# FNet mixing and gated layers on one Trainium2 core: 65-row tiles for the odd folds, a padded row 512, earlier weight loads and a new place table

## The chip, the cores and the metric

The kernel runs on one core of a Trainium2 chip. The metric is the device time of that core in microseconds (us), the median of 3 runs. The core's engines are the matrix engine (PE), VectorE (DVE), ScalarE (ACT), GpSimd (POOL) and SyncE (SP), which here issues nearly all the transfers, in program order on one queue.

## The reference

Two equal layers on x of 2048 rows and 640 columns, all in float32; the three weights are the same in both layers and have 1728 inner columns.

```python
for layer in range(2):
    z = layernorm(x)
    x = x + (Cr @ (z @ Hr.T) - Ci @ (z @ Hi.T))      # real part of the DFT over the rows of the DFT over the columns
    z = layernorm(x)
    x = x + (sigmoid(z @ w_gate) * (z @ w_up)) @ w_down
```

Cr and Ci are the 2048 x 2048 cosine and sine matrices of the sequence, Hr and Hi the 640 x 640 ones of the columns.

## The kernel before

**Layout.** The function `folded` does the work. It uses the symmetries of the DFT matrices, and tests the given matrices for them beside the work; a general version stands by for other inputs and isn't run here. One large buffer in the on-chip memory, `big` in the profile, holds 406 units of 128 float32 columns. Everything that comes and goes is a run of units in it: `take(n, name)` hands one out, `drop(name)` gives it back. Where each of the 913 takes lies is written in the table PLACES, in program order. A take over a place that was in use a moment before waits, by semaphores, for the last reader of the old content, so the table decides which jobs wait for which.

**Products in float16 halves.** Most operands are split into a high and a low float16 part (`split`, lines 234 to 239: ScalarE makes the high part at L237, VectorE the low one at L239), and each product is three matmuls, high x high, high x low and low x high (`PASSES`). In the opening of layer 1 the sequence step works on float32 directly.

**The mixing step.** The rows of x come in 4 quarters of 512, each as four groups GA to GD of 128 rows. Column c and column 640 - c, and row s and row s + 1024 or 2048 - s, are added and subtracted first. What comes of it are an even fold FE of 321 columns and an odd fold FO of 320 columns; the 321st column of FO is cleared (`zero_odd`, line 848, in the opening, and line 680 in `fold_join`), so that both have one width in memory. Quarter 1 (`SP`) has besides a lone row, row 512, which is its own mirror image. It is kept apart as `row`, float32 on partition 0 (lines 601 to 605), is scaled in `fold_row` and split to `fw`, and meets the cosine matrix' row 512, `cx` raw and `c512` split.

The sequence step (`sequence32`, line 812, float32, for layer 1; `sequence`, line 759, float16, for layer 2) multiplies a fold, as weights, by a sequence matrix, as moving data of 256 or 257 columns, and so transposes it: the fold's columns land on partitions, in three tiles d. `KT` (line 758) gives for each parity r the first column and the number of columns of these tiles: 128, 128 and 65 for the even fold, 128, 128 and 64 for the odd one. Row 512 is added by further matmuls with one row of contraction (K = 1): one per tile in float32 (L832), three per tile in float16 (L793).

The hidden step contracts over those same tiles, whose row counts are again `KT[r]`:

```python
def product(ps, ph, r, at, m):
    for d, (_, n) in enumerate(KT[r]):
        w = held["h", r, d].f16[:n]
        for zp, wps in PASSES:
            z = held["z", ph, d].parts[zp][:n]
            for wp in wps:
                nc.tensor.matmul(ps[:m, :EC], z[:, at : at + m], w[:, 384 * wp : 384 * wp + EC],
                                 start=(d == 0 and zp == HI and wp == HI), stop=(d == ND // 2 and zp == LO))
```

The matmul is L917, and its shape in the profile is weights n x m and moving data n x 321. One `hidden` step is two products of 9 matmuls. There are 8 of them per layer, and `hidden_middle` besides, with a single column (m = 1) for output row t = 512, which `evict_middle` reads from partition 0 of the result. The matrices' rows come from `load_wh` (first layer) and `load_wh_again`.

**The gated step.** `gate_up` (L1123) and the later `seven` and `four` (L1167, tile by tile of the inner columns, index j) make the gate and up products; ScalarE evicts them (L1171). `seven` and `four` use sums and differences of blocks, in the manner of Strassen, so that fewer products are needed; the weights' sums are made in layer 1 (`load_sums`, `make_sums`, `split_sums`, `keep_sums`) and kept in device memory (`kept_S`, `kept_G`). The down product of layer 1's first half is done directly (`down`, L1309). The others use seven forms of pairs of weight tiles (`stage`, L1423), which layer 1 prepares during its second half: for each of the six pairs n, `load_forms` loads the raw weights (L1333, L1335) to `fr`, `make_forms` makes four differences on GpSimd (L1342 and the lines after) in `ft`, `split_forms` splits three forms from `fr` (part 0) and four from `ft` (part 1) on ScalarE and VectorE, and `keep_forms` stores them to `kept_f`.

The rows for the second half of the gated step come in four row pairs i. For each, `pair_apply` normalizes, `pair_combine` makes the sums, `pair_parts` splits them in four parts (L516 on ScalarE, L517 on VectorE), and `pair_transpose` issues the transposing transfers (L533).

**What orders the work.** The first 99 us (the mixing step of layer 1 and the start of the gated step) are a list written by hand, OPENING. After that the matrix engine's steps stand in one list with planned durations; T is the sum of these, and `when(t, f, ...)` puts a job of another engine into the program at planned time t. The planned times only set the program order: within an engine, and on the queue of transfers, work goes in that order, whatever it waits for. T = 0 is at about 98.9 us of the profile. Three planned times are used below: `d0`, the start of the down product of the first half (T = 146.3, about 247 us), `s1`, the start of the second half's `seven` (T = 235.4, about 336 us), and 96 + 11.5 k, the turn of the k-th sequence matrix. These turns belong to layer 1: `load_c`, `split_c` and `stored_c` prepare the 8 sequence matrices and row 512 in float16 for layer 2, where `load_c_again` and `load_c512_again` load them.

## Time and profile before

| | |
|---|---|
| runs | 1110.03, 1113.09, 1113.80 us |
| median | 1113.09 us |
| span of the profiled execution | 1111.5 us, 17471 instructions |
| matrix engine busy | 1091.5 us (98%), 6295 instructions |
| VectorE | 828.8 us (75%) |
| ScalarE | 570.9 us (51%) |
| GpSimd | 152.1 us (14%) |

The profile is of one execution, the times are of others. In a line of the timeline stand the start in us, the duration, the engine, the source line, the operation, the tile written and read with its shape, and how often it came in a row; in brackets the idle time before it and what ended that. For a matmul the shape `65*128 65x321` means weights of 65 rows and 128 columns and moving data of 65 rows and 321 columns. "SPq" is the queue of transfers. In a row of the windows view come the stretch, its length, the time of the matrix engine, of its weight loads, of VectorE, ScalarE and GpSimd (each with the number of instructions), the granted clock of the matrix engine, the share of the DMA engines and GB/s. Matmuls overlap in the records, so the time that one takes is read from the distance of the starts.

### The profile page before, as it was taken

Reading aid. Unit: us, or ns where it says so; the run is one execution under the profiler, and the core shown is the slowest. Engines: PE = TensorE matmul, PEld = TensorE weight load, DVE = VectorE, ACT = ScalarE, POOL = GpSimd, SP = SyncE. Lnnn points to the kernel's source line nnn. Section 1 sums busy time; section 2 is a strip of 40 time slices with the busy share of each in tenths; the row PEclk is TensorE's granted clock in tenths of the full one; section 3 lists DMA queues with packets and bytes.
Section 4 is the critical chain, followed back from the end, with each engine's and each line's share of the span. In section 5 each row is a group of like instructions: output and inputs, shape, how many; then the busy total and the mean of one; then the engine's idle time right before and its main releaser. Section 6 shows DMA issues by size and latency. Waiting matters only on the chain.

```text
span 1111.5 us, 17471 instructions
## 1 busy us (share of the span) xinstructions
PE 1091.5 (98%) x6295; PEld 621.8 (56%) x6295; DVE 828.8 (75%) x1608; ACT 570.9 (51%) x1108; POOL 152.1 (14%) x245
## 2 busy tenths in 40 slices
PE   6999999999998999999999999999999999999997
PEld 3667444447774444447777744444677544444775
DVE  8986789867556999769886659885896356777952
ACT  7766447765333656546224544477553245455520
POOL 3110151321323243000020000012000010000010
PEclk9999999999999999999999999999999999999999
DMA  9413764365888778856833039645669756666611
GB/s 278 159 49 70 197 205 173 106 208 156 209 232 263 249 237 246 239 163 212 242 110 119 1 49 192 188 165 164 200 175 202 221 184 198 211 196 191 225 61 63
DMA packets 183080, 194.69 MB, mean 175 GB/s; under 512 B 76459, under 2 KB 145476, under 8 KB 182984
## 3 DMA queue, kind: packets, MB, share of 16 engines
q1 hardware_dynamic: 182344, 190.86, 58.7%
q0 software_dynamic: 640, 2.62, 0.6%
q8 instruction: 51, 0.84, 0.3%
q14 instruction: 45, 0.37, 0.1%
HBM read 145.29 MB, written 31.90 MB: 159 GB/s over the span
## 4 chain that ended last, share of the span: by engine, by line
PE 83%; DVE 6%; DMA 5%; SPq 3%; ACT 1%; issue 1%; POOL 1%; DVEq 0%; POOLq 0%; ACTq 0%
PE acc L1167 38%; PE acc L1423 17%; PE acc L1123 14%; PE acc L917 4%; PE acc L1404 3%; PE acc L1276 2%; DMA big<-in_wu 2%; PE acc L829 2%; PE acc L786 1%; SPq L533 1%; SPq L1495 1%; DMA big<-in_wd 1%; DVE big L239 1%; DMA big<-in_x 1%; DMA big<-in_ct 1%
## 5 line engine op out<-in xcount | busy, mean ns | idle before, releaser
L1167 PE MATMUL acc<-big 128*128 128x512 f16 x2160 | 469.5, 380 | 3.9 <-ACT big L1171 3.2
L1167 PEld LDWEIGHTS <-big 128*128 128x128 f16 x2160 | 211.6, 98 | 260.3 <-issue 6.1
L1423 PE MATMUL acc<-big 128*128 128x320 f16 x1512 | 213.2, 299 | 0.4 <-DVE big L1297 0.4
L1171 ACT ACTIVATE big<-acc 128x512 f32<-128x512 f32 x160 | 94.0, 592 | 181.7 <-PE acc L1167 169.8
L1423 PEld LDWEIGHTS <-big 128*128 128x128 f16 x1512 | 147.9, 98 | 58.5 <-issue 0.6
L1123 PE MATMUL acc<-big 128*128 128x512 f16 (+1 forms) x900 | 156.5, 337 | 0.0
L1123 PEld LDWEIGHTS <-big 128*128 128x128 f16 x900 | 87.8, 98 | 68.2 <-issue 0.8
L1474 ACT ACTIVATE big<-big 128x768 f32<-128x768 f32 (+6 forms) x106 | 79.0, 746 | 64.5 <-DVE big L1504 24.9
L239 DVE SCALAR_TENSOR_TENSOR big<-big 128x640 f16<-128x640 f32 (+7 forms) x94 | 75.7, 829 | 19.1 <-ACT big L237 19.0
L1297 DVE SCALAR_TENSOR_TENSOR big<-acc,big 128x320 f32<-128x320 f32 x112 | 53.1, 486 | 48.7 <-PE acc L1404 25.8
L1309 PE MATMUL acc<-big 128*128 128x320 f16 x656 | 89.3, 299 | 0.0
L237 ACT ACTIVATE big<-big 128x640 f16<-128x640 f32 (+9 forms) x94 | 63.8, 707 | 48.9 <-DMA big<-in_ct 21.9
L1384 DVE TENSOR_TENSOR big<-big 128x512 f16<-128x512 f32 x126 | 85.5, 689 | 4.4 <-ACT big L1383 4.4
L1383 ACT ACTIVATE big<-big 128x512 f16<-128x512 f32 x126 | 72.8, 616 | 18.4 <-DVE big L1261 10.1
L1309 PEld LDWEIGHTS <-big 128*128 128x128 f16 x656 | 64.2, 98 | 25.1
L1217 DVE TENSOR_TENSOR big<-big,acc 128x512 f32<-128x512 f32 x40 | 27.3, 682 | 41.0 <-PE acc L1167 26.0
L516 ACT ACTIVATE big<-big 128x384 f16<-128x384 f32 (+2 forms) x56 | 36.1, 667 | 35.4 <-DVE big L501 18.5
L1174 ACT ACTIVATE big<-big 128x512 f32<-128x512 f32 x80 | 49.7, 621 | 8.2 <-DVE big L1217 7.2
L517 DVE TENSOR_TENSOR big<-big 128x384 f16<-128x384 f32 (+2 forms) x56 | 42.6, 773 | 13.6 <-ACT big L516 13.5
L386 POOL DMA_INDIRECT out<-big,rows x8 | 8.8, 1097 | 309.2 <-DVE big L1297 168.0
L1395 DVE TENSOR_TENSOR big<-big 128x512 f32<-128x512 f32 x72 | 50.2, 699 | 0.1
L917 PE MATMUL acc<-big 128*128 128x321 f16 (+3 forms) x324 | 48.6, 300 | 0.0
(195 smaller groups left out, 1193.5 us busy)
## 6 DMA issues: line engine op xcount, KB each, us to landing
big<-in_ct SPq DMA_DIRECT2D x256, 128.0 KB
big<-kept_f SPq DMA_DIRECT2D x63, 320.0 KB
big<-kept_S SPq DMA_DIRECT2D x33, 512.0 KB
big<-kept_w SPq DMA_DIRECT2D x33, 320.0 KB
big<-in_ct SPq DMA_DIRECT2D x32, 256.0 KB
big<-kept_G SPq DMA_DIRECT2D x21, 320.0 KB
kept_S<-big SPq DMA_DIRECT2D x13, 512.0 KB
big<-in_wg SPq DMA_DIRECT2D x19, 320.0 KB
```

What stands on the lines that cost most here:

```text
L237: nc.scalar.activation(dh, src, AF.Copy, scale=s)
L239: nc.vector.scalar_tensor_tensor(dl, src, s, dh, op0=OP.mult, op1=OP.subtract)
L917: nc.tensor.matmul(ps[:m, :EC], z[:, at : at + m], w[:, 384 * wp : 384 * wp + EC], start=(d == 0 and zp == HI and wp == HI), stop=(d == ND ...
L1123: nc.tensor.matmul(ps, w[wp][:, d * P : (d + 1) * P], xt[:, xp, :], start=(d == 0 and wp == HI and xp == HI), stop=(d == ND - 1 and wp == LO))
L1167: nc.tensor.matmul(ps, wt, xt, start=start and n == 0, stop=n == len(todo) - 1, skip_group_check=not start)
L1171: nc.scalar.activation(dst, ps, AF.Copy)
L1297: nc.vector.scalar_tensor_tensor(xe, ps[:, :EH], CB, xe, op0=OP.mult, op1=OP.add)
L1309: nc.tensor.matmul(held["pd", i, e][0][:, :EH], held["t", half, j].parts[hp][:, i * P : (i + 1) * P], held["w", 2, j].parts[wp][:, e * EH ...
L1383: nc.scalar.activation(h, v, AF.Copy)
L1384: nc.vector.tensor_tensor(l, v, h, op=OP.subtract)
L1423: nc.tensor.matmul(ps[:, :EH], a[n][hp][:, i * P : (i + 1) * P], w[n][:, wp], start=fresh and m == 0, stop=m == len(todo) - 1, skip_group_ ...
L1474: nc.scalar.activation(v, v, AF.Square, accum_out=new_sum()[:p])
```

## The change

1. **Third tile of the odd folds.** `KT` gives both parities 128, 128 and 65 rows. On the sequence side the new row is the cleared 321st column; on the hidden side `load_wh` loads one more row of the odd matrix.
2. **Row t = 512.** `hidden_middle` takes 97 columns that end at the one wanted, instead of one column, and `evict_middle` reads partition 96 instead of partition 0.
3. **Row 512, padded.** `row` and `cx` are cleared on all 128 partitions on GpSimd before they are filled, and the float32 matmul in `sequence32` takes 128 rows instead of one. In float16 the parts go onto spare partitions of one cleared tile: in `fw` the high part on rows 0 and 64 and the low part on row 32, in `c512` the high part on rows 0 and 32 and the low part on row 64. One matmul with 128 rows gives the three products at once. `fw` takes 2 units instead of 3, `c512` in layer 2 takes 3 instead of 5, and is loaded by a clear and three transfers instead of one transfer. `sequence` no longer stores `c512` itself; `stored_c512` still does.
4. **Planned times, all in layer 1.** The third and fourth row pairs go from d0 + 50 and d0 + 63 to d0 + 47 and d0 + 57. The sequence matrices are loaded 4 us of plan earlier, row 512 3 us earlier. The raw weights of pair 0 are loaded at s1 - 30 instead of s1 - 12; its differences and splits stay where they are.
5. **PLACES** is a new table for the takes of this program. It is cut here to its first and last lines.

```diff
--- before.py
+++ after.py
@@ -72,39 +72,39 @@
 PLACES = """
-115 380 366 221 234 326 146 85 141 307 80 372 151 90 122 367 401 275 190 272 377 138 258 352 161 108 166 289
...
-301 372 148 332 160 336 368 276 169 203 280 295 344 208 176 243 225"""
+405 80 404 403 81 86 91 96 400 101 395 106 111 116 121 126 390 131 134 384 387 381 140 143 374 369 364 359 354
...
+273 327 208 343 402 172 367 336 237 332"""
@@ -601,7 +601,9 @@
         if i == SP:
 
             if "row" not in held:
-                take(6, "row")
+                v = take(6, "row").f32[:, :EC]
+                if not steps:
+                    nc.gpsimd.memset(v, 0.0)
             on.tensor_copy(held["row"].f32[0:1, 384 * k : 384 * k + EC], e[0:1, 1])
 
     def fold_power(i, k0, k1, on=nc.gpsimd):
@@ -649,10 +651,13 @@
             nc.vector.scalar_tensor_tensor(f[0:1, :EC], f[0:1, 384 : 384 + EC], t[0:1, GD, 19:20], f[0:1, :EC],
                                            op0=OP.mult, op1=OP.add)
         if n == 2:
-            nc.scalar.activation(take(3, "fw").f16[0:1, :EC], f[0:1, :EC], AF.Copy)
+            w = take(2, "fw").f16[:, :EC]
+            nc.gpsimd.memset(w, 0.0)
+            for p in (0, 64):
+                nc.scalar.activation(w[p : p + 1], f[0:1, :EC], AF.Copy)
         if n == 3:
-            w = held["fw"].f16
-            nc.vector.tensor_tensor(w[0:1, 384 : 384 + EC], f[0:1, :EC], w[0:1, :EC], op=OP.subtract)
+            w = held["fw"].f16[:, :EC]
+            nc.vector.tensor_tensor(w[32:33], f[0:1, :EC], w[0:1], op=OP.subtract)
             drop("row")
 
     def drop_rev():
@@ -743,7 +748,9 @@
         nc.sync.dma_start(kept_part(take_c(r, i), r), kept["c", r, i])
 
     def load_c512():
-        nc.sync.dma_start(take(5, "cx").f32[0:1, : SB + 2], ct[0, SB : SB + 1, : SB + 2])
+        v = take(5, "cx").f32[:, : SB + 2]
+        nc.gpsimd.memset(v, 0.0)
+        nc.sync.dma_start(v[0:1], ct[0, SB : SB + 1, : SB + 2])
 
     def split_c512(do=ALL):
         h, l = (held["c512"] if "c512" in held else take(5, "c512")).parts
@@ -752,9 +759,12 @@
             drop("cx")
 
     def load_c512_again():
-        nc.sync.dma_start(kept_part(take(5, "c512"))[0:1, :, :257], kept["c512",])
-
-    KT = ((0, P), (P, P), (2 * P, EC - 2 * P)), ((0, P), (P, P), (2 * P, EH - 2 * P))
+        v = take(3, "c512").f16
+        nc.gpsimd.memset(v[:, :257], 0.0)
+        for p, q in ((0, 0), (32, 0), (64, 1)):
+            nc.sync.dma_start(v[p : p + 1, :257], kept["c512",][:, q])
+
+    KT = (((0, P), (P, P), (2 * P, EC - 2 * P)),) * 2
 
     def sequence(i, tp):
 
@@ -787,17 +797,12 @@
                                              start=(i % 2 == 0 and r == 0 and xp == HI and cp == HI),
                                              stop=(i % 2 == 1 and r == 1 and xp == LO))
                     if i == SP and tp == EV and r == 0:
-                        xv, cps = held["fw"].f16[0:1], held["c512"].parts
-                        for xp, cs in PASSES:
-                            for cp in cs:
-                                nc.tensor.matmul(o, xv[:, 384 * xp + c0 : 384 * xp + c0 + n], cps[cp][0:1, :257],
-                                                 start=False, stop=False)
+                        nc.tensor.matmul(o, held["fw"].f16[:, c0 : c0 + n], held["c512"].f16[:, :257],
+                                         start=False, stop=False)
 
         def post():
             if i == SP and tp == EV:
                 drop("fw")
-                if ("c512",) not in kept:
-                    keep(kept_part(held["c512"])[0:1, :, :257], "c512")
                 drop("c512")
             summed.add((i, tp))
             if {(i, EV), (i, OD)} <= summed:
@@ -829,7 +834,7 @@
                     nc.tensor.matmul(o[:n], xv[:, c0 : c0 + n], moving(r), start=i % 2 == 0 and r == 0,
                                      stop=i % 2 == 1 and r == 1)
                     if i == SP and tp == EV and r == 0:
-                        nc.tensor.matmul(o[:n], held["row"].f32[0:1, c0 : c0 + n], held["cx"].f32[0:1, 0 : SB + 1 : 2],
+                        nc.tensor.matmul(o[:n], held["row"].f32[:, c0 : c0 + n], held["cx"].f32[:, 0 : SB + 1 : 2],
                                          start=False, stop=False)
 
         def post():
@@ -892,7 +897,7 @@
 
     def load_wh(r, d):
         s = take(3, "hr", r, d).f32
-        n = KT[1][d][1]
+        n = KT[r][d][1] - (r == 0 and d == 2)
         nc.sync.dma_start(s[:n, :EC], wh[r, d * P + 1 : d * P + 1 + n, :EC])
         if r == 0 and d == 2:
             nc.sync.dma_start(s[n : n + 1, :EC], wh[r, 0:1, :EC])
@@ -926,12 +931,14 @@
 
         return 18 * 0.1362, mm, lambda: None
 
+    MID = 96
+
     def hidden_middle():
 
         def mm():
             pair = held["py", NB] = bank_pair()
             for r in range(2):
-                product(pair[r][0], r, r, SB, 1)
+                product(pair[r][0], r, r, SB - MID, MID + 1)
 
         return 18 * 0.1362, mm, lambda: None
 
@@ -968,11 +975,11 @@
     def evict_middle(do=ALL):
         (a, ka), (b, kb) = held["py", NB]
         if 0 in do:
-            nc.scalar.activation(pair_of(take(6, "mid"))[0:1, 1], b[0:1, :EC], AF.Copy, scale=CY)
+            nc.scalar.activation(pair_of(take(6, "mid"))[0:1, 1], b[MID : MID + 1, :EC], AF.Copy, scale=CY)
         if 1 in do:
             v = pair_of(held["mid"])[0:1]
-            nc.vector.scalar_tensor_tensor(v[:, 0], a[0:1, :EC], CY, v[:, 1], op0=OP.mult, op1=OP.subtract)
-            nc.vector.scalar_tensor_tensor(v[:, 1], a[0:1, :EC], CY, v[:, 1], op0=OP.mult, op1=OP.add)
+            nc.vector.scalar_tensor_tensor(v[:, 0], a[MID : MID + 1, :EC], CY, v[:, 1], op0=OP.mult, op1=OP.subtract)
+            nc.vector.scalar_tensor_tensor(v[:, 1], a[MID : MID + 1, :EC], CY, v[:, 1], op0=OP.mult, op1=OP.add)
             del held["py", NB]
             free_bank(ka, kb)
 
@@ -1835,7 +1842,7 @@
                 when(s0 + (24, 50)[q] + 4 * i, pair_stats, 1, i, q, True)
             when(s0 + 70 + q, quad_scale, 2 + q)
         for i in range(TB):
-            u = d0 + ((2, 20, 50, 63) if first else (6, 20, 46, 56))[i]
+            u = d0 + ((2, 20, 47, 57) if first else (6, 20, 46, 56))[i]
             when(u, pair_apply, 1, i, 0, True)
             when(u + 0.5, pair_apply, 1, i, 1, True)
             when(u + 2, pair_combine, 1, i)
@@ -1883,11 +1890,11 @@
             for n in range(NB):
                 for r in range(2):
                     u = 96 + 11.5 * (2 * n + r)
-                    when(u, load_c, r, n)
+                    when(u - 4, load_c, r, n)
                     when(u + 5, split_c, r, n, (0,))
                     when(u + 5.7, split_c, r, n, (1,))
                     when(u + 7, stored_c, r, n)
-            when(96 + 3, load_c512)
+            when(96, load_c512)
             when(96 + 6, split_c512)
             when(96 + 8, stored_c512)
             for j in range(5, NF):
@@ -1925,7 +1932,7 @@
                 when(d0 - 8 + 1.6 * j, split_w, 2, j)
             for n in range(PAIRS):
                 u = s1 - 12 + 21.5 * n
-                when(u, load_forms, n)
+                when(u if n else s1 - 30, load_forms, n)
                 when(u + 13, make_forms, n)
                 for k in range(2):
                     when(u + 14 + 7 * k, split_forms, n, k)
```

62 rows, old and new, of the table PLACES are left out of this document.

## The prediction

> **What bounds the kernel now.** I read the page first, then the matrix engine's waits, then the timelines of the queue, of ScalarE and of VectorE around each long wait.
>
> ```profile
> span 1111.5 us, 17471 instructions
> PE 1091.5 (98%) x6295; PEld 621.8 (56%) x6295; DVE 828.8 (75%) x1608; ACT 570.9 (51%) x1108; POOL 152.1 (14%) x245
> PE acc L1167 <- ACT big L1171: 3.2, 2, 2.6
> PE acc L1167 <- DMA big<-big: 0.6, 1, 0.6
> ```
>
> The matrix engine is busy for 98% of the span. A microsecond taken from it, or a wait of it that goes, shortens the kernel by as much, unless the next operand comes too late. The waits view names only a few; the two above lie in the first layer and are what the moved steps aim at. So there are two kinds of gain: time inside the matmul stream, and these waits.
>
> **Part 1: the odd folds' third tile, 64 rows to 65.** The starts of matmuls around such a tile, one row from each of five narrow windows of the timeline:
>
> ```profile
> 592.65 0.57 PE L917 MATMUL acc<-big 65*128 65x321 f16 x3
> 593.06 0.44 PE L917 MATMUL acc<-big 128*128 128x321 f16 x2
> ...
> 593.75 0.68 PE L917 MATMUL acc<-big 128*128 128x321 f16 x3
> 593.98 0.58 PE L917 MATMUL acc<-big 64*128 64x321 f16 x3
> 594.49 0.28 PE L786 MATMUL acc<-big 128*128 128x256 f16 x1
> ```
>
> Three matmuls on 65 rows take from 592.65 to 593.06, 0.41 us, 0.137 each: the pitch of the full tiles. The last full matmul before the 64-row tile takes from 593.75 to 593.98, 0.23, and the three of 64 rows from there to 594.49, 0.51. Four matmuls in 0.74 us instead of 0.55: 0.19 us goes into entering and leaving the 64-row form, about half at each end, and nothing into 65 rows. The grouped view by form counts the occurrences:
>
> ```profile
> L917 PE MATMUL acc<-big 64*128 64x321 f16 x48 | 9.3, 300 | 0.0
> L917 PE MATMUL acc<-big 64*1 64x321 f16 x6 | 1.1, 295 | 0.0
> ```
>
> 54 matmuls in threes are 18 tiles: 18 x 0.19 = 3.4 us, half of it in each layer. The added row is zero on the sequence side, since the odd parts' last column is cleared already, so the sum is unchanged. The middle product, now 97 columns instead of 1, keeps its 18 matmuls; by the same shape change it may win a little more, which I leave out (0 to 0.19, one more such switch).
>
> **Part 2: row 512.** In the second layer three one-row matmuls per tile become one on 128 rows, the spare rows being zero. The chain of waits there:
>
> ```profile
> 578.55 2.30 PE acc L786 x21
> 580.85 0.43 PE acc L793 x3
> ...
> 583.68 8.31 PE acc L786 x75
> ```
>
> From 580.85 to 583.68 there are 9 one-row matmuls and 12 others, 2.83 us. Afterwards there are 3 + 12, at the pitch of the first row (2.30 / 21 = 0.11): 1.64. That is 1.2 us less. In the first layer the count stays, and only the shape changes (two rows of this chain, and a later row with the float32 pitch):
>
> ```profile
> 37.01 0.65 PE acc L832 x2
> ...
> 41.11 0.61 PE acc L829 x2
> 41.74 0.61 ACT big L237
> ...
> 45.24 2.53 PE acc L829 x10
> ...
> 53.02 5.62 PE acc L829 x24
> ```
>
> From 37.01 to 41.72 are 16 matmuls, 4.71 us; at 5.62 / 24 = 0.234 they would take 3.75. So 1.0 us. It counts, because the eviction at 41.74 follows these matmuls and the chain goes on through it to the matmuls at 45.24.
>
> The padding adds clearing work on GpSimd. The long row (514 columns) is cleared in program order after the iotas and ahead of the clears of the odd folds, and VectorE waits for those:
>
> ```profile
> 0.72 0.20 POOL L242 MEMSET dsum<- 128x128 f32 x1 [0.29 <-POOLq L2140]
> 0.86 0.15 POOL L243 MEMSET cmax<- 128x64 f32 x1
> 0.95 0.13 POOL L244 MEMSET wmax<- 128x42 f32 x1
> 11.79 0.84 DVE L594 TENSOR_TENSOR big<-big 128x640 f32<-128x640 f32 x1 [1.10 <-POOL big L851]
> ```
>
> 128 columns hold GpSimd 0.14 us, 64 hold it 0.09; on that line 514 take 0.4 to 0.5 (an estimate from these rows; bounds 0.14 and, in proportion, 0.56). VectorE works on from there with hardly a pause up to the first sequence matmuls, so I charge 0.4 in full. The DMA of that row, which now waits for the clear, stands on the queue behind all the x loads and two matrices, and its turn comes after the clear. The row is loaded twice more. In the first layer's weight stage the clear may meet four of GpSimd's sums, and the queue, with stores and one matrix load behind it, would stand for 0 to 5.8 us (four times 1.45, the longest such operation quoted below); the next matmuls want nothing of these, so 0. For the second layer it becomes three small transfers behind a clear, in a stage in which GpSimd has next to nothing to do and for data wanted a stage later: 0.
>
> In the fold of quarter 1 for the second layer, ScalarE now waits for a clear on GpSimd too, and that is queued behind the four differences of weight pair 4:
>
> ```profile
> 430.41 1.45 POOL L1342 TENSOR_TENSOR big<-big 128x320 f32<-128x320 f32 x1 [11.22 <-DMA kept_f<-big]
> 431.02 0.46 ACT L652 ACTIVATE big<-big 1x321 f16<-1x321 f32 x1
> ```
>
> As it stands, GpSimd would be free after four such, 5.8 us at most, by 436.2, and ScalarE, with the matmul evictions behind it, would stand up to 5.2 us. But GpSimd started late only because the differences' place was still being stored. Counting down the new table, that tile lies at 235, over the first part of pair 3 and no longer over the second, which is stored 7 us of plan later. GpSimd is then done by about 430. Bounds 0 to 5.2; I take 0, the row being nearer to that once the 11.22 is gone.
>
> **Part 3: what is moved.** The long wait, on the queue, on ScalarE and on the matrix engine:
>
> ```profile
> 317.05 1.48 DVE L517 TENSOR_TENSOR big<-big 128x768 f16<-128x768 f32 x1
> 327.68 6.90 SPq L533 DMA_TRANSPOSE big<-big  x1
> 337.28 0.46 SPq L1335 DMA_DIRECT2D big<-in_wd  x1
> 339.22 0.43 SPq L1333 DMA_DIRECT2D big<-in_wd  x1
> 343.33 1.00 ACT L237 ACTIVATE big<-big 128x960 f16<-128x960 f32 x1 [4.88 <-DMA big<-in_wd]
> 344.24 0.58 ACT L1171 ACTIVATE big<-acc 128x512 f32<-128x512 f32 x1
> 336.30 6.00 PE L1167 MATMUL acc<-big 128*128 128x512 f16 x27 [0.55 <-DMA big<-big]
> 344.87 5.51 PE L1167 MATMUL acc<-big 128*128 128x512 f16 x18 [2.57 <-ACT big L1171]
> 344.87:347.81 2.94, 2.94 (x8) 0.99 (x8) 2.91 (x6) 2.48 (x4) 1.10 (x2) 0.50 0.54 185
> ```
>
> The weights of pair 0 are issued at 337.28 to 339.22, behind the last transposes; they land at 343.33, ScalarE stands 4.88 us in front of them, and the eviction behind it holds the matmuls for 2.57 us. After that the granted clock is 0.50 for 2.94 us, half of it lost: 1.5. At the change of stage another 0.55 went on the last transposes.
>
> After the change the load comes 18 us of plan earlier, behind the third row pair's transposes and ahead of the fourth's. The third pair's parts come 3 us, the fourth's 6 us of plan sooner, and so ahead of the splits of the weight sums of matrices 4 and 5, behind which the third pair's last part stood until 317.05. The new table puts parts 2 and 3 over parts 0 and 2, so each waits for a transpose to land; with 5 to 7 us for a transpose I count the third out at about 314, the weights issued by 317, the fourth out at 326 and landed at 328, where the matmuls come at 333. Nothing else is late there: 0.55 + 2.57 + 1.5 = 4.6 us go. The cover left is some 5 us.
>
> The raw matrix loads come 4 us of plan sooner, which meets one wait:
>
> ```profile
> 211.84 0.41 SPq L719 DMA_DIRECT2D big<-in_ct  x1
> 216.04 0.67 ACT L237 ACTIVATE big<-big 128x514 f16<-128x514 f32 x1 [3.41 <-DMA big<-in_ct]
> 219.28 2.97 PE L1167 MATMUL acc<-big 128*128 128x512 f16 x13 [0.66 <-ACT big L1171]
> ```
>
> The load still stands behind a store that waits for a split, but ahead of two others: about 1 us sooner, enough for the 0.66. I take 0.4.
>
> A rule speaks against one term. The Trainium skill (TensorE: Matmul & The Clock Gate, Part 1, What's actually happening) has the clock halved only after at least one idle window of about 3.4 us. By it the 2.57 us wait would not bring the 0.50, and the sum below would be 8.7 in place of 10.2. Here the trace disagrees: the slow stretch begins at the very matmul that waited, and I go by the row.
>
> **Sum:** 3.4 + 1.2 + 1.0 - 0.4 + 4.6 + 0.4 = 10.2. The profiled span of 1111.5 becomes 1101.3; the median of the runs, 1113.09, lies 1.6 above that span, so 1102.9.
>
> **The rivals.**
> The opening keeps its length: VectorE is packed there, and the earlier matmuls only wait. Then the first layer's half of 3.4 and the 1.0 are lost: 10.2 - 2.7 = 7.5, so 1105.6. For it: VectorE's and GpSimd's chain sets much of the opening, as at 11.79. Against: from 45.24 on the chain of waits runs through the matmuls.
> The wait at 344 only changes its owner, a transpose or the load being late for another reason: 4.6 lost, 1107.5. Against: 5 us of cover.
> The half clock is not tied to that wait and stays: 1.5 lost, 1104.4; only a stretch of 0.50 after no wait would speak for it. The Trainium skill's page named above would have it so.
> The padded forms switch all the same: 3.4 + 1.2 + 1.0 lost, 1108.5. The rows with 65 speak against it.
> Slower: the new table lays weight pairs 1, 3 and 5 on the pair just before, so their loads wait for its last split, and the queue holds the next tiles' weights behind them.
>
> ```profile
> 390.49 0.44 SPq L1335 DMA_DIRECT2D big<-in_wd  x1
> 395.18 1.49 DVE L239 SCALAR_TENSOR_TENSOR big<-big 128x1280 f16<-128x1280 f32 x1
> 396.94 0.33 SPq L1096 DMA_DIRECT2D big<-kept_G  x1
> ```
>
> Pair 3's load, at 390.49, would wait until 396.7, 6.2 us, and tile 6's weights go from 396.94 to 403.1. Tile 6 starts at 408.5 (18 matmuls of tile 0 from 344.87, then 54 of 0.216 per tile). A load took 4.1 us above (339.22 to 343.33), so the cover is 11.6 - 4.1 = 7.5, and it decides from a hold of 7.5 us on. With VectorE twice as far behind, a hold of 12.5 costs 5 us of waiting and 1.5 of half clock at each of three places: 19.5, so 1122.4.
>
> **How the numbers follow.** The forecast has 0.63, the opening 0.17, the wait that moves 0.09, the clock 0.04, the switching forms 0.02, the slower case 0.05. The likeliest is 1102.9. Down, 1098.5: the middle product's 0.19 and the whole 0.66 at 219 give 1102.4, and the runs spread over 3.8. Up, 1108.5 takes in every case but the slower one. About 0.3%, 3.3 us, is what a measurement of this kernel can tell from no change: the bound for faster is 1109.8. All cases but the slower lie below it; mixtures of them and a partial hold leave 0.04 for the same and 0.04 for slower: 0.92, 0.04, 0.04.
>
> **What would show it.** Right: no form with 64 rows or one row in the view by form; in the second layer 18 hidden matmuls at one even pitch; the sequence step of quarter 1 shorter by 1.2; pair 0's weights issued before the fourth transposes; no wait of ScalarE for them, and the clock at 1.00 right through 330 to 350. Wrong: waits of the matrix engine for weights between 350 and 480, ScalarE waiting for GpSimd near 425, or the matmuls at 45 starting no earlier than now.

## The result and the profile after

The changed kernel takes 1105.12 us (median of 4 runs, 1103.99 to 1106.11); the kernel before takes 1113.31 (4 runs, 1110.03 to 1113.80). The ratio is 0.9936, with a 95% interval of 0.9917 to 0.9955: 8.2 us less, where I had forecast 10.2. The profiled execution took 1106.03.

```profile
span 1104.2 us, 17528 instructions
...
PE 1084.0 (98%) x6289; PEld 626.3 (57%) x6289; DVE 830.2 (75%) x1608; ACT 572.9 (52%) x1109; POOL 154.6 (14%) x250
```

The span is 7.3 shorter, and the matrix engine's busy time 7.5 (1091.5 to 1084.0). Below, line numbers of the changed kernel are 2 to 10 higher than those of the kernel before from line 604 on (L1171 is now L1178, L1167 is L1174), and those of an experiment can differ by one more.

The third tiles first, in the view by form. There is no form with 64 rows and none with one column:

```profile
L922 PE MATMUL acc<-big 128*128 128x321 f16 x192 | 31.5, 300 | 0.0
L922 PE MATMUL acc<-big 65*128 65x321 f16 x96 | 18.4, 299 | 0.0
L922 PE MATMUL acc<-big 128*97 128x321 f16 x24 | 3.9, 299 | 0.5 <-ACT big L971 0.5
L922 PE MATMUL acc<-big 65*97 65x321 f16 x12 | 2.3, 299 | 0.0
```

The place of the long wait, in the windows view and in the timelines of the queue and of ScalarE:

```profile
330.00:350.00 20.00, 20.00 (x99) 9.52 (x98) 18.36 (x37) 10.03 (x18) 6.00 (x11) 1.00 0.71 241
```

```profile
299.25 7.21 SPq L533 DMA_TRANSPOSE big<-big  x1
...
307.66 0.38 SPq L1342 DMA_DIRECT2D big<-in_wd  x1
...
314.00 5.13 SPq L533 DMA_TRANSPOSE big<-big  x1
...
333.76 0.99 ACT L237 ACTIVATE big<-big 128x960 f16<-128x960 f32 x1
```

The matrix engine is busy for all of 330 to 350 at the full clock. The weights of pair 0 are issued at 307.66, between the third transposes (299.25) and the fourth (314.00), and ScalarE takes them at 333.76 without standing. So far the change did what the prediction says. But behind the opening the matrix engine's waits have four rows that the kernel before doesn't have:

```profile
PE acc L1174 <- ACT big L1178: 1.9, 1, 1.9
...
PE acc L1174 <- DMA big<-big: 0.9, 1, 0.9
...
PE acc L796 <- DVE big L239: 0.6, 1, 0.6
PE acc L922 <- ACT big L971: 0.5, 1, 0.5
```

The timelines of the engines at these places, in the order of time:

```profile
427.31 1.54 DVE L682 TENSOR_TENSOR big<-big 128x642 f16<-128x642 f32 x2
428.97 1.08 ACT L1178 ACTIVATE big<-acc 128x512 f32<-128x512 f32 x2 [2.22 <-DVE big L682]
429.61 0.59 PE L1174 MATMUL acc<-big 128*128 128x512 f16 x2 [1.90 <-ACT big L1178]
...
579.60 1.65 DVE L682 TENSOR_TENSOR big<-big 128x642 f16<-128x642 f32 x2
581.16 3.07 DVE L239 SCALAR_TENSOR_TENSOR big<-acc,big 128x512 f16<-128x512 f32 x5
581.90 2.78 PE L796 MATMUL acc<-big 128*65 128x256 f16 x24 [0.56 <-DVE big L239]
...
608.70 0.83 ACT L438 ACTIVATE big<-big,rowt 128x640 f32<-128x640 f32 x1
609.53 0.75 ACT L971 ACTIVATE big<-acc 128x321 f32<-128x321 f32 x2
610.00 2.63 PE L922 MATMUL acc<-big 128*97 128x321 f16 x18 [0.53 <-ACT big L971]
...
850.82 7.16 SPq L533 DMA_TRANSPOSE big<-big  x1
860.07 2.10 PE L1174 MATMUL acc<-big 128*128 128x512 f16 x9 [0.90 <-DMA big<-big]
```

At 428.97 ScalarE's eviction writes to a place of which VectorE (L682) has just read the odd fold of quarter 1. At 581 a matmul needs a bank of the accumulator that VectorE empties only after splitting the folds of quarter 3; at 609 the same holds for ScalarE, which is busy with the statistics of a row tile. At 859 the last transposes land late. With what the restarts cost, these are 2.06, 0.72, 0.69 and 1.07: 4.54 us.

To see what was gained, I took each distance between two starts of matmuls, less the pitch of its form, and added these up by cause, in the two profiled executions:

| term | forecast | measured |
|---|---|---|
| third tiles and middle product | 3.4 | 1.77 + 1.89 = 3.66 |
| row 512, layer 2 | 1.2 | 1.3 |
| row 512, opening | 1.0 | 1.06 |
| GpSimd's clear in the opening | -0.4 | -0.47 |
| GpSimd's first instructions 0.50 sooner | 0 | 0.50 |
| waits at 335 and 342, half clock | 4.6 | 0.71 + 2.73 + 1.43 = 4.87 |
| waits at 206 and 219 | 0.4 | 0.29 + 0.82 = 1.11 |
| new waits | 0 | -4.54 |
| sum | 10.2 | 7.49 |

What the clear costs stands in two rows, of GpSimd and of VectorE, which waits for the clears behind it:

```profile
11.16 0.52 POOL L752 MEMSET big<- 128x514 f32 x1
...
11.75 0.84 DVE L594 TENSOR_TENSOR big<-big 128x640 f32<-128x640 f32 x1 [1.29 <-POOL big L856]
```

GpSimd's next instruction starts at 11.62, 0.47 us behind the clear's start. VectorE's L594 starts no later than before (11.79) only because GpSimd began its chain at 10.40 and not at 10.90 in this execution. Over all the profiled executions here it begins between 10.07 and 11.56, with no order by kernel.

### The profile page after: what moved, and what is told of

The parts are those of the page before. It is cut to its first block, busy times and chain, and to the rows that moved or that the text cites. A ratio compares the mean times of both kernels' runs of the same rounds, so it can differ in the third digit from the quotient of the medians.

```text
span 1104.2 us, 17528 instructions
## 1 busy us (share of the span) xinstructions
PE 1084.0 (98%) x6289; PEld 626.3 (57%) x6289; DVE 830.2 (75%) x1608; ACT 572.9 (52%) x1109; POOL 154.6 (14%) x250
## 4 chain that ended last, share of the span: by engine, by line
PE 87%; DVE 8%; issue 2%; DMA 1%; ACT 1%; POOL 0%; SPq 0%; DVEq 0%; POOLq 0%; ACTq 0%
PE acc L1174 36%; PE acc L1430 17%; PE acc L1130 14%; PE acc L1316 8%; PE acc L922 4%; PE acc L1411 2%; PE acc L1283 2%; PE acc L834 2%; DVE big L642 1%; DMA big<-big 1%; DVE quad L424 1%; DVE big L239 1%; PE acc L796 1%; DVE big L1509 1%; DVE big L594 0%
## 5 line engine op out<-in xcount | busy, mean ns | idle before, releaser
L1174 PE MATMUL acc<-big 128*128 128x512 f16 x2160 | 467.8, 379 | 2.8 <-ACT big L1178 1.9
L1174 PEld LDWEIGHTS <-big 128*128 128x128 f16 x2160 | 211.3, 98 | 257.8 <-issue 3.5
L1178 ACT ACTIVATE big<-acc 128x512 f32<-128x512 f32 x160 | 94.0, 593 | 191.9 <-PE acc L1174 167.5
L1481 ACT ACTIVATE big<-big 128x768 f32<-128x768 f32 (+6 forms) x106 | 79.0, 745 | 53.2 <-DVE big L1511 17.0
L1509 DVE TENSOR_TENSOR big<-big 128x512 f32<-128x512 f32 x64 | 46.2, 722 | 5.9 <-DMA big<-in_ct 5.7
L1402 DVE TENSOR_TENSOR big<-big 128x512 f32<-128x512 f32 x72 | 50.1, 697 | 0.1
L439 POOL TENSOR_SCALAR rowt<-rowt 128x1 f32<-128x1 f32 x24 | 13.0, 540 | 242.4 <-ACT big L437 242.4
```

What stands on the lines that cost most here:

```text
L1174: nc.tensor.matmul(ps, wt, xt, start=start and n == 0, stop=n == len(todo) - 1, skip_group_check=not start)
L1178: nc.scalar.activation(dst, ps, AF.Copy)
L1481: nc.scalar.activation(v, v, AF.Square, accum_out=new_sum()[:p])
L1509: nc.vector.tensor_tensor(bd[:, :, 1], bd[:, :, 0], bd[:, :, 1], op=same)
```

## The experiments

My theory: the gains are all there, and each of the four new waits has its own cause, two by places of the new table, two by the order of jobs on VectorE and ScalarE. The rival: these engines and the queue have no slack at those places, so a wait that is taken away only changes its owner.

**e1, 65 rows alone,** on the kernel before.

```diff
-    KT = ((0, P), (P, P), (2 * P, EC - 2 * P)), ((0, P), (P, P), (2 * P, EH - 2 * P))
+    KT = (((0, P), (P, P), (2 * P, EC - 2 * P)),) * 2
...
-                product(pair[r][0], r, r, SB, 1)
+                product(pair[r][0], r, r, SB - MID, MID + 1)
```

> The kernel before with 65 rows in the odd third tiles and 97 columns in the middle product, and nothing else. My account: the hidden steps lose the 1.8 us of layer 1 and the 1.9 us of layer 2 that their 64-row and one-column forms cost, and about 0.6 of it comes back as a wait of the middle product for ScalarE's eviction near 609, as in the changed kernel. Net 3.1 us, a span of about 1108.4. Rival: that wait belongs to another part of the change (ScalarE made late by the sums' evictions), so it is absent here and the net is 3.7, a span of 1107.8; the trace shows which, by a wait ahead of the middle product.

1109.40 against 1112.09: ratio 0.9976 (0.9966 to 0.9985), span 1106.8. The hidden steps lost 1.77 and 1.89 us, and the middle product now waits:

```profile
613.72 2.49 PE L917 MATMUL acc<-big 128*97 128x321 f16 x17 [0.47 <-ACT big L966]
```

So that wait comes with the 65 rows and 97 columns and not with another part. The span fell by 1.6 more than forecast, nearly all of it the half clock behind the wait at 342 (1.43), which this execution didn't have (see e12).

**e2, the padded row 512 alone,** on the kernel before and with its table.

```diff
-                        for xp, cs in PASSES:
-                            for cp in cs:
-                                nc.tensor.matmul(o, xv[:, 384 * xp + c0 : 384 * xp + c0 + n], cps[cp][0:1, :257],
+                        nc.tensor.matmul(o, held["fw"].f16[:, c0 : c0 + n], held["c512"].f16[:, :257],
...
+            nc.gpsimd.memset(w, 0.0)
+            for p in (0, 64):
+                nc.scalar.activation(w[p : p + 1], f[0:1, :EC], AF.Copy)
```

> The kernel before with the padded row 512 alone. My account: 1.2 us in the opening and 1.3 in the second layer's sequence step, of which 0.7 comes back because the third bank of quarter 2 waits for VectorE's eviction of the sums. Net 1.8, a span of about 1109.7. Rival: the clear on GpSimd delays VectorE in the opening by the 0.4 that I predicted, a span of 1110.1; and if the wait for VectorE belongs to another part of the change, 0.7 less.

1111.13 against 1112.09: ratio 0.9992 (0.9978 to 1.0005), no measurable difference, span 1111.6. The 1.06 and 1.3 us are in the trace. Against them stand three waits: 0.64 at 588 and 1.26 at 435, below, and 0.87 more than before at the change of stage (1.58 at 334). The opening began 0.37 later, and the waits at 206, 217 and 342 were 1.05 shorter in all. The profiled execution, 1113.37, is one of the slowest of these runs (median 1111.13), so the waits need not be as long in the others.

```profile
433.08 0.36 POOL L655 MEMSET big<- 128x321 f16 x1
433.48 0.97 ACT L657 ACTIVATE big<-big 1x321 f16<-1x321 f32 x2 [1.70 <-POOL big L655]
436.94 1.24 PE L1172 MATMUL acc<-big 128*128 128x512 f16 x5 [1.10 <-ACT big L1176]
...
589.15 2.78 PE L796 MATMUL acc<-big 128*65 128x256 f16 x24 [0.48 <-DVE big L239]
```

The wait for VectorE's eviction is there with the padded row alone. And with the old table the clear of `fw` stands behind the differences of pair 4 on GpSimd, and ScalarE behind the clear: the cost that I had bounded by 0 and 5.2 and taken as 0. In the changed kernel the same clear runs at 415.19, 8 us before ScalarE asks for it, because the new table and the moves let pair 4's differences start sooner (at 409.96; at 411.52 in e6, which has none of the rows' parts; at 428.44 here).

**e3, the place of one eviction** (and 25 takes that had to make room).

```
take 420, y of tile 8, first half:  159 -> 325   (off the odd fold of quarter 1)
```

> The changed kernel, with 26 takes of the second half of layer 1 at other places, so that the eviction at 428.97 no longer lies over the odd fold of quarter 1. My account: the 1.9 us wait of the matrix engine at 427 (2.06 with the slow restart) comes from that place, so it goes: span 1104.2 - 2.1 = 1102.1. Rival: ScalarE and VectorE are late there whatever the place, and the wait only changes its owner: 1104.2.

1105.24, ratio 0.9933 (0.9920 to 0.9946), span 1104.1: nothing gained. The wait at 427 is gone, and a longer one stands 12 us later:

```profile
432.56 0.57 SPq L257 DMA_DIRECT2D kept_e<-big  x1
441.69 1.08 ACT L1179 ACTIVATE big<-acc 128x512 f32<-128x512 f32 x2 [4.28 <-DMA kept_e<-big]
442.33 1.02 PE L1175 MATMUL acc<-big 128*128 128x512 f16 x4 [2.40 <-ACT big L1179]
```

The next tile's eviction lies over the even parts of quarter 1, whose store is issued at 432.56 and holds their place until 441.6. That place is the new table's own; in the changed kernel ScalarE waits there too:

```profile
439.94 1.09 ACT L1178 ACTIVATE big<-acc 128x512 f32<-128x512 f32 x2 [2.41 <-DMA kept_e<-big]
```

There the matrix engine has no wait. That it had lost its 1.9 us just before may be why, but this isn't shown: in e6 it lost 1.80 before and still waited 0.31, in e8 it lost 1.31 and didn't wait. So the rival was right about this run, but by a second place and not for lack of slack; e5 tells these apart.

**e4, the places of layer 2's down stage** (32 takes).

```
takes 736, 737, 738, 742, split forms of stages 4 and 5:  402, 398, 394, 360 -> 321, 222, 305, 402
take 740, weights of stage 5:                             307 -> 252
```

> The changed kernel, with 32 takes of layer 2's down stage at other places, so that the split forms of stages 4 and 5 no longer lie over tiles of which VectorE reads shortly before. My account: ScalarE then squares the test rows 3 us sooner, the queue's test loads are held 3 us less, the third and fourth transposes go out sooner, and the wait of 0.90 us at 859 (1.07 with the restart) goes: 1104.2 - 1.1 = 1103.1. Rival: the transposes are late because the matrix engine arrives sooner and the queue's own traffic is the same, so the wait stays: 1104.2.

1104.85, ratio 0.9936 (0.9923 to 0.9948), span 1102.8. The rows that answer, of the changed kernel and then of this run:

```profile
809.95 0.63 ACT L1390 ACTIVATE big<-big 128x512 f16<-128x512 f32 x1 [2.69 <-DVE big L1391]
...
812.69 0.83 ACT L1481 ACTIVATE big<-big 128x768 f32<-128x768 f32 x1
```

```profile
808.82 0.84 ACT L1482 ACTIVATE big<-big 128x768 f32<-128x768 f32 x1 [0.31 <-DVE big L1512]
...
808.81 2.86 SPq L1503 DMA_DIRECT2D big<-in_ct  x4
811.72 5.36 SPq L1379 DMA_DIRECT2D big<-kept_f  x3
```

ScalarE's square of the test rows (L1481, here L1482) goes out 3.9 us sooner, 3.1 counted from the start of the stage (779.68 and 778.92), as I had it, and the test loads behind it too. But the stage's weights (L1379) now stood 4 us on the queue, since I had laid take 740 over a tile that VectorE still read. The wait at 859 fell from 0.90 to 0.33. That can't be put down to the places, since the same wait was 0.39 in another execution of the changed kernel (e11) and absent in e3, e7 and e8 with its old places in this stage. What this run shows is ScalarE's 3.1 us; that the late weights ate up the gain behind it is likely and not shown.

**e5, both, with a table that leaves room** (127 takes moved, these among them). Nearly no eviction, load or split in these two stages lies now over what a store, a transpose or VectorE leaves only a few us of plan before.

```
take 420, y of tile 8:                  159 -> 366
take 411, even parts of quarter 1:      349 -> 273      (from under take 430, y of tile 9, at 354)
takes 736, 737, 738, 742, split forms:  402, 398, 394, 360 -> 210, 364, 222, 317
take 740, weights of stage 5:           307 -> 347
```

> The changed kernel with 127 takes at other places, in the second half of layer 1 and in layer 2's down stage, none of which now lies over something that a store, a transpose or VectorE leaves only a few us of plan before (the two runs before had each put a new reuse of that kind in the place of the old one: a tile over a fold still being stored at 439, a stage's weights over a tile that VectorE still read at 812). My account: the waits at 427 and at 859 come from places alone, so both go and none comes: span 1104.2 - 2.1 - 1.1 = 1101.0. Rival: ScalarE and VectorE have no slack there, and some other job holds them by as much: 1104.

1102.41 against 1112.81: ratio 0.9910 (0.9895 to 0.9925), span 1100.1. Both waits are gone and none came. The second half of layer 1 runs through, and the transposes in layer 2 are back where they were with the old table; the fourth of them in the kernel before, and in this run with the matmul that needs it:

```profile
855.04 6.35 SPq L533 DMA_TRANSPOSE big<-big  x1
```

```profile
843.93 6.39 SPq L534 DMA_TRANSPOSE big<-big  x1
...
855.97 1.24 PE L1175 MATMUL acc<-big 128*128 128x512 f16 x5
```

Here the last transposes are issued 5.6 us before the matrix engine arrives (855.97 less 850.32), in the kernel before 6.2, in the changed kernel 1.2. (The expectation has one thing wrong: the fold being stored at 439 was the changed kernel's own place, as e3 shows, not one that I had put there.)

**e6, the moves and the new table alone,** without the two rows' parts (four takes of the table lie elsewhere).

```diff
-            u = d0 + ((2, 20, 50, 63) if first else (6, 20, 46, 56))[i]
+            u = d0 + ((2, 20, 47, 57) if first else (6, 20, 46, 56))[i]
...
-                    when(u, load_c, r, n)
+                    when(u - 4, load_c, r, n)
...
-                when(u, load_forms, n)
+                when(u if n else s1 - 30, load_forms, n)
```

> The kernel before with the new planned times and the new table (two takes elsewhere for their larger size), without 65 rows and without the padded row. My account: the waits at 206, 218, 335 and 342 go with the half clock, 0.29 + 0.82 + 0.71 + 2.73 + 1.43 = 6.0, and the table's waits at about 431 and 867 come, 2.1 + 1.1: span 1111.5 - 6.0 + 3.2 = 1108.7. Rival: the two new waits come from the rows' parts making the matrix engine early, so they are absent: 1105.5.

1109.21 against 1112.81: ratio 0.9972 (0.9962 to 0.9982), span 1107.3. The four old waits are gone. The first new one is there with none of the rows' parts, and so is the one for the store; one of 0.66 at 1081 stands in no other run:

```profile
431.00 11.81 PE L1168 MATMUL acc<-big 128*128 128x512 f16 x54 [1.80 <-ACT big L1172]
443.13 3.18 PE L1168 MATMUL acc<-big 128*128 128x512 f16 x14 [0.31 <-ACT big L1172]
```

The one at 867 is not: the last transposes are issued 2.4 us ahead of the matrix engine, and that was enough (see e11).

**e7, the load of pair 0 put back.**

```diff
-                when(u if n else s1 - 30, load_forms, n)
+                when(u, load_forms, n)
```

> The changed kernel with the raw weights of pair 0 loaded at s1 - 12 again, everything else as changed. My account as predicted: the earlier load is what takes the wait of the matrix engine at 337 away, so 2.6 and, if the wait is as long as before, 1.5 of half clock come back: span 1106.8 to 1108.3. Rival: the earlier row pairs do it alone, since the fourth transposes are issued at 314 and the load behind them at about 322 would land by 328, ahead of the split at 333.8: 1104.2.

1104.90, ratio 0.9932 (0.9918 to 0.9946), span 1102.5: the same as with the load moved. The weights go behind the fourth transposes and are there in time:

```profile
315.53 5.10 SPq L534 DMA_TRANSPOSE big<-big  x1
...
325.97 0.46 SPq L1343 DMA_DIRECT2D big<-in_wd  x1
...
333.29 0.99 ACT L238 ACTIVATE big<-big 128x960 f16<-128x960 f32 x1
```

ScalarE starts at 333.29, with no wait in front. So the earlier load is not what took the wait away.

**e10, the row pairs put back,** the load moved.

```diff
-            u = d0 + ((2, 20, 47, 57) if first else (6, 20, 46, 56))[i]
+            u = d0 + ((2, 20, 50, 63) if first else (6, 20, 46, 56))[i]
```

> The changed kernel with the third and fourth row pairs at d0 + 50 and d0 + 63 again, and the raw weights of pair 0 still at s1 - 30. The run with the load put back showed no wait near 337, so one of two accounts of the 4.9 us must give way. First account: each of the two moves is enough for the wait for the weights, and only the wait for the last transposes at the change of stage needs the row pairs: 0.7 us come back near 331, none near 337, a span of 1104.9. Second account: only the row pairs matter, since the load waits on the queue for whatever the transposes wait for: both waits come back, 0.7 and 2.0 to 2.7, a span of 1107 to 1108.

1106.00 against 1112.46: ratio 0.9943 (0.9930 to 0.9957), span 1103.8.

```profile
306.37 0.37 SPq L1343 DMA_DIRECT2D big<-in_wd  x1
...
323.16 6.62 SPq L534 DMA_TRANSPOSE big<-big  x1
...
331.97 14.41 PE L1175 MATMUL acc<-big 128*128 128x512 f16 x66 [0.69 <-DVE big L1305]
```

The wait at the change of stage is back with 0.85 us, restart included, and the one for the weights is not. The profile names VectorE for it. But in the changed kernel the same matmul starts at 331.72, while VectorE still has three of these four evictions to end (331.52 to 332.79), so the likelier cause is the last transposes, which were still being issued until 329.78. Each move alone is enough for the wait for the weights; only the row pairs help at the change of stage.

**e8, the order of two jobs in layer 2's mixing step,** all places kept.

```diff
-    run_at(end + 3, [(fold_join, 3, ALL, (n,)) for n in range(3)])
+    run_at(end + 3, [(fold_join, 3, ALL, (0,))])
+    run(he + 2.5, [(fold_join, 3, ALL, (n,)) for n in (1, 2)])
...
-    run(he + 15, [(evict_hidden, 1, 1), (norm_stats_act, 3), (norm_scale, 2, 2)])
-    run(he + 16, [(evict_hidden, 2, 1), (transpose_pe, 0), (transpose_pe, 1)])
+    run(he + 15, [(evict_hidden, 1, 1)])
+    run(he + 16, [(evict_hidden, 2, 1), (norm_stats_act, 3), (norm_scale, 2, 2), (transpose_pe, 0), (transpose_pe, 1)])
```

> The changed kernel, all places kept, with two jobs of layer 2's mixing step later in the program: the splits of quarter 3's folds behind the eviction of the first sums, and the statistics of row tile 3 behind the eviction of hidden tile 2. My account: the waits at 581 and 609 are VectorE and ScalarE serving other jobs first, so both go: span 1104.2 - 0.72 - 0.69 = 1102.8. Rival: the moved jobs are needed as early as they stood, and the matrix engine waits for them a little later (sequence step of quarter 3 near 587, gate products near 620): 1104.2 or more.

1103.51 against 1112.81: ratio 0.9922 (0.9908 to 0.9936), span 1101.5. The wait at 609 is gone and the one at 581 fell from 0.72 to 0.30, with none later in the mixing step.

**e9, places and order together.** Its edits are those of e5 and e8.

> The changed kernel with the places of the run with 127 takes moved and with the two jobs of layer 2's mixing step put later, as in the run before. My account: the four new waits of the changed kernel have four separate causes, two places and two orders, so the gains add: 1100.1 - 0.42 at 581 - 0.69 at 609, a span of 1099.0. Rival: with the places cleared, another job is next in line by as much, and the span stays at 1100.

1101.58 against 1112.46: ratio 0.9904 (0.9888 to 0.9920), span 1099.2. Of the four new waits 0.3 us are left. It is the fastest of all the kernels here, 3.2 us below the changed kernel (e11, on the same chip).

**e11, the changed kernel again.**

> The changed kernel once more, to see which of its waits stand in every execution. My account: the wait of 1.9 us at 427 is there again (an eviction over the fold of quarter 1 must always wait), the one at 859 need not be: in the five runs with these places the last transposes end 1.2 to 2.4 us ahead of the matrix engine, against 5.6 to 6.2 with the old places, and it waits only where that is under 2.0. Rival: the wait at 859 is fixed too, and its absence in other runs came from their other edits: 0.90 again.

1104.81 against 1112.46: ratio 0.9932 (0.9918 to 0.9945), span 1102.6. The waits view:

```profile
PE acc L1174 <- ACT big L1178: 1.8, 2, 1.6
...
PE acc L1174 <- DMA big<-big: 0.4, 1, 0.4
```

The wait at 427 is 1.60 here, that at 859 0.39 in place of 0.90. Over the seven runs with these places the last transposes are issued 1.2 to 2.4 us ahead of the matrix engine, and it waits 0.90 at 1.19, 0.39 at 1.67, 0.23 at 1.82 and not at all from 2.0 on. The table took 4 of the 6 us of cover; the execution decides on the rest.

**e12, the kernel before again.**

> The kernel before once more. The 4.9 us that I put on the waits at 335 and 342 and on the half clock come from one execution. My account: the waits are there in every execution, 0.7 to 1.6 at 335 and 2.0 to 2.7 at 342 (the two runs with the old order had 1.5 and 2.0, 1.6 and 2.3), and the half clock follows only where the idle time is as long as the 2.57 of the first profile: the idle times of 1.86 here and of 2.16 and 2.40 elsewhere had none. Rival: the half clock belongs to this kernel at this place whatever the wait, or came by chance, which a wait of under 2.4 with a half clock, or one of 2.57 without, would show.

1111.76 against 1111.57: ratio 1.0005 (0.9995 to 1.0014), span 1108.5, which is 3 us less than in the first profile. Of these, 1.43 are the half clock behind the wait at 342, and 1.33 are another stretch of half clock, in the opening. From the first sequence matmul to the first hidden one it is 21.38 us in the first profile and 20.05 here. The windows view, of the first profile and then of this one:

```profile
27.20:30.40 3.20, 3.20 (x8) 2.30 (x9) 3.10 (x11) 3.17 (x9) 1.90 (x3) 0.50 0.97 316
```

```profile
27.20:30.40 3.20, 3.20 (x16) 2.45 (x15) 3.06 (x13) 3.17 (x9) 1.89 (x3) 1.00 0.91 258
```

The changed kernel's first profile, e1, e2 and e3 have this stretch too, the other eight runs don't. With the padded row it costs 1.0 us (20.31 against 19.30). So the spans that I expected from 1104.2 were 1.0 too long for the runs without it, and what e4, e5 and e8 fell by beyond the wait that was aimed at is in part this.

The matmuls behind the longer wait of this execution:

```profile
342.30 7.93 PE L1167 MATMUL acc<-big 128*128 128x512 f16 x36 [1.93 <-ACT big L1171]
```

Both waits, at 334 and 340 here, are there again, 0.43 and 2.09 with their restarts, and no half clock. (A wait of 0.45 for a load at 453 stands in no other run.) But the expectation leans on a misreading: in e2 the clock did halve, 1.1 us after the matmuls went on. The windows view, of e2 and then of e3 behind its longer wait:

```profile
345.00:348.40 3.40, 3.40 (x10) 1.16 (x8) 3.33 (x8) 1.49 (x2) 0.19 (x1) 0.52 0.55 188
```

```profile
442.30:445.70 3.40, 3.37 (x16) 1.56 (x16) 3.38 (x5) 3.40 (x7) 0.87 (x1) 1.00 0.90 320
```

So 2.57 and 2.16 of idle time were followed by the half clock, 2.40, 1.93, 1.90 and 1.86 were not. In the opening, the idle time in front of the first sequence matmul is 1.81 to 1.98 in every run, and five of the 14 have the half clock within 2 us behind it. The length alone doesn't decide.

## Why the prediction was right and where it was wrong

**The terms inside the matmul stream** were right within 0.3 us each (3.4, 1.2, 1.0 against 3.66, 1.3, 1.06). The 1.06 is between two executions that both have the half clock in the opening; between two without it, e12 and e11, the padded row gains 0.75 there (20.05 to 19.30). In the opening the hidden steps of layer 1 gave what was counted: 51.42 us from the first hidden matmul to the first of 512 columns (47.62 to 99.04), 49.56 in the changed kernel (46.58 to 96.14) and 49.51 in e1. So the rival that the opening keeps its length is out, though its 1105.6 is nearly the measured time; and so is that of the padded forms that switch all the same.

**The clear of the opening** cost what I charged: 0.47 us for 0.4, on the path that I named. In three of the four runs without the clear, VectorE's L594 waits for GpSimd and starts 0.88 us behind GpSimd's first iota; in all ten with it the distance is 1.35. From there VectorE has no pause of over 0.1 us up to the first sequence matmul, some 14.5 us later in each of these. In the changed kernel's first profile the cost was hidden by luck, GpSimd having begun 0.50 us sooner.

**The moves** took away what I said, 4.87 for 4.6. The reason was only half right: I gave the wait for the weights to the earlier load, and e7 and e10 show that either move does it. I had the fourth transposes out at 326 and 5 us of cover; they were out at 319, 12.6 us ahead of the matmul at 331.72. The half clock's part, 1.43, was a matter of the execution: in the two executions of the kernel before it was there once. The 206 and 219 waits were under-counted, 0.4 for 1.11; the first of them I had left out, and since it is gone in e2 as well, it needs none of the moves to go.

**What failed** is the step that judged the new table. "Nothing else is late there" held at the change of stage itself, where the matrix engine is busy all through 330 to 350. But the sum has no term for what is late elsewhere, and 4.54 us were: 3.13 by places, 1.41 by order. By itself this error makes 1107.4 of my 1102.9. That is inside the range only because its upper end, 1108.5, was set by other rivals; none of them had these waits. The measured sum is nearer to the forecast by terms that I had counted too low, 0.7 at the waits at 206 and 219 and 0.6 in the others, and by the 0.50 of GpSimd's chance start. I had looked for takes over things that transfers were still to fill or empty ahead of the long wait, and for the clear, and counted the cover of the weight pairs' loads. I had not asked the same of the evictions: one over a fold that VectorE reads late (427, 1.9 us, e3 and e5), and not of layer 2, where the program is unchanged but its places are not (859, 0 to 1.1 us by the execution). The rival for the slower side was about the right cause, the table, at the wrong place: no matmul waited for weights between 350 and 480. How narrow it was, the old table shows: there another eviction lay over the same fold, ScalarE waited 1.87 us at 435.78 (2.45 in e12), and the matrix engine not at all.

**What comes late next** is a question that I asked of the stalls and not of the gains inside the stream: the faster sequence and hidden steps arrive at banks that VectorE and ScalarE have not yet emptied (e1, e2), and 1.4 us of 6.0 came back, of which e8 and e9 won 1.1 by order alone. These two waits need no new table.

## What to carry to other kernels

A hand-made table of places is part of the schedule: a change of it can cost as much as a moved job, and in stages that the change doesn't touch, so each take should be asked who last used the place and how late that engine runs against the plan there. When an experiment takes a wait away and the time stays, look whether a second wait of the same kind stood behind it before you conclude that there is no slack. And a gain inside a full stream of matmuls is only worth what the engines that empty the accumulator's banks can follow. Single profiles are best compared after a look at their clock rows: one stretch of half clock in the opening was worth 1.0 to 1.3 us here, in kernels before and after the change alike.

## What the runs showed of the hardware

A clock halved for about 3 us after a pause of under 2.6 us was not what I expected, nor that it is so uncertain: it followed pauses of 2.57 and 2.16 us, once at once and once 1.1 us late, and didn't follow one of 2.40. In the opening a pause of 1.8 to 2.0 us, the same in every run, was followed by it in 5 of 14. It cost 1.0 to 1.5 us each time. The Trainium skill (TensorE: Matmul & The Clock Gate, Part 1, What's actually happening) says that the activity is watched in free-running windows of about 3.4 us; pauses that fall differently into such windows would give what is seen, though no pause here filled a whole one, as its rule of at least one idle window would have it. No run here shows the windows.
